# Retention attention and a two-layer product on one core: attention of the later blocks placed at a fixed pace in the plan, smaller groups, another cost for late loads

## The chip, the core and the metric

The kernel runs on one core of a Trainium2 chip. A core has five engines with a queue each: TensorE (PE, matrix products; its weight loads are listed apart as PEld), VectorE (DVE), ScalarE (ACT), GpSimd (POOL) and SyncE (SP), which here issues nearly all transfers between HBM and the on-chip memory SBUF. Products land in PSUM, which this kernel handles as eight banks. Each engine works through its own list in order and waits on semaphores for the others.

The metric is the device time of one execution in microseconds. Before the change the median of three runs is 235.52 us (235.09 to 236.05).

## The reference

Inputs are q, k, v of 4 batches, 8 heads, 768 positions and 64 dimensions, a decay `lam` for each head, and two weight matrices of 512x2048 and 2048x512. Attention is causal without a softmax: position i weighs position j by lam^(i-j). It is written in blocks with a running state:

```python
intra = (qb @ kb.T * Dmask) @ vb                 # Dmask[i,j] = lam**(i-j), i >= j
inter = (qb * lam_pow) @ kv_state
out[block] = intra + inter
kv_state = lam_block * kv_state + (kb * rev_pow).T @ vb
```

The result, as 3072 rows of 512, goes through two products: `h = x @ w_in`, `g = h * sigmoid(h)`, `out = g @ w_out`.

## The kernel before

The 3072 rows are 24 blocks `u` of 128 positions, six to a batch. Per block, attention does this:

- DVE scales q (`qs`, L315) and k (`ks`, L369) by powers of lam; PE transposes both (`tr_ps`, L327 and L389); ACT or DVE copies the transposes to SBUF (`qT`, `kTz`). Except for blocks 0, 1, 22 and 23 (`plain`), q is loaded and scaled for two blocks together, in two halves.
- PE makes the scores (`st_ps`, L415, two halves of four heads), and DVE masks them (`st_sb`, L424).
- v is copied into a padded tile (`vz`). PE makes the block's output (`x_ps`, L453, and L457 for the part from the state), ACT or DVE copies it to `xt`.
- Unless the block ends a batch, PE makes the state's increment (`d_ps`), DVE adds the state (`y`, L500), POOL decays it (`Xz`, `Xf`, L229).

Blocks below `WIDE` = 8 use a padded form of k (`kp`, L361): eight transposes into 128x1024 (L377) with one copy of 1024 columns, eight d_ps products of 64 columns (L480) and one y. The others use four transposes, two copies of 512 columns on 64 partitions, four d_ps products of 128 columns (L484) and two y.

The products work on groups of blocks: `xts[g]` holds one, two or four blocks. The first product (L545) of a group streams 128 columns per block, so 128, 256 or 512; each bank of four 128x128 tiles takes one SiLU on ACT (`g`, L554). A group of any size takes 64 first products. The second product (L573) takes 16 products of 512 columns for each block and needs the whole group's `g` and all of w_out. DVE or ACT copies the result (`o_sb`, L226 and L224) and SP stores it. The last block's second product is split in two halves of 256 columns (L612).

The weights arrive in eight pieces each (`wst`, L269 and L272) and are cast to bf16 on DVE or ACT (`w_in_bf`, `w_out_bf`). SP issues all loads in one written order: k, q, v of the first blocks, w_in between blocks 1 and 6, then w_out, then blocks 8 to 23.

What order each engine's list has is decided at build time by a planner (`Plan`). Every step is an `op` with the engines that may do it and a cost for each, the steps it depends on, a priority, and rings of buffers that it takes and frees. `run` repeatedly takes the step that can start first by its own clock, with fixed latencies between engines, and the instructions are then written out by those start times. The planner's times do not exist at run time: an engine starts an instruction when its semaphores allow it. `after` adds a delay to the time at which a step's dependencies count as done. The step `late`, a step on no engine, makes a load count as landed 4.0 us later for blocks from 8 on. Where the planner sees PE idle in the first 90 us for long enough, `idle` puts in products of zeros (`warm_ps`, L650).

Of the kernel before, what the change touches and what calls it, by code (L numbers as in the profile page):

```python
# [13 lines left out]
class Plan:  # L14
# [9 lines left out]
        self.ops = []  # L24
        self.rings = {}

    def op(self, engines, deps, fn, prio, alloc=(), frees=(), after=0.0):


        o = dict(engines=engines, deps=[d for d in deps if d is not None], fn=fn, prio=prio,  # L30
                 alloc=list(alloc), frees=list(frees), id=len(self.ops), end=None, slots={}, after=after)
        self.ops.append(o)
        return o

# [12 lines left out]
    def run(self, start, idle=None):  # L47
        INF = float("inf")
        free = dict(start)
        users = {}  # L50
        for o in self.ops:
            o["wait"] = len(o["deps"])
            for d in o["deps"]:
                users.setdefault(d["id"], []).append(o)
        ready = [o for o in self.ops if o["wait"] == 0]
        out = []
        while ready:
            pick = {}
            for o in ready:
                slots = max([self.slot(a)[1] for a in o["alloc"]] or [0.0])  # L60
                if slots == INF:
                    continue
                if "SP" in o["engines"]:
                    slots += self.AHEAD
                at = {e: max([free[e] if e != "NONE" else 0.0, slots] + [o["after"] + d["end"] + (self.LAT[d["eng"]] if d["eng"] != e else 0.0)
                                                 for d in o["deps"]]) for e in o["engines"]}
                home = next(iter(at))
                e = min(at, key=lambda e: at[e] + o["engines"][e] + (self.AWAY if e != home else 0.0))
                pick.setdefault(e, []).append((at[e], o))
            if not pick:  # L70
                raise RuntimeError("no operation can start")

            e, l = min(pick.items(), key=lambda kv: min(x[0] for x in kv[1]))
            t0 = min(x[0] for x in l)
            t, o = min((x for x in l if x[0] <= t0 + 0.02), key=lambda x: (x[1]["prio"], x[0], x[1]["id"]))
            if idle is not None and e == "PE":
                idle(free[e], t, out)
            o["eng"], o["start"], o["end"] = e, t, t + o["engines"][e]
            free[e] = o["end"]
            for a in o["alloc"]:  # L80
                i, _ = self.slot(a)
                o["slots"][a] = i
                self.rings[a]["next"] += 1
                self.rings[a]["free"][i] = INF
            for owner, a in o["frees"]:
                self.rings[a]["free"][owner["slots"][a]] = o["end"] + self.LAT[e]
            ready.remove(o)
            out.append((t - (self.AHEAD if e == "SP" else 0.0), len(out), o))
            for u in users.get(o["id"], ()):
                u["wait"] -= 1  # L90
                if u["wait"] == 0:
                    ready.append(u)
        left = [o for o in self.ops if o["end"] is None]
        if left:
            raise RuntimeError(f"{len(left)} operations never start")
        return sorted(out, key=lambda x: x[:2])
# [3 lines left out]
def kernel(  # L100
# [15 lines left out]
    NU = B * NB  # L116
# [4 lines left out]
    KI = DM // 128  # L121
    KO = DFF // 128
    HB = BLK // 2
    WIDE = 8

    ctx.enter_context(tc.manual_schedule())
    const = ctx.enter_context(tc.tile_pool(name="const", bufs=1))
# [3 lines left out]
    plan = Plan()  # L131
# [9 lines left out]
    def sb(o, name, shape, dtype, tag=None):  # L141
        return work.tile(shape, dtype, tag=tag or name, bufs=BUFS[tag or name], name=name)

    def bank(o, name, shape, dtype):
        return ps.tile(shape, dtype, tag=f"b{o['slots']['bank']}", name=name + "_ps")
# [65 lines left out]
    w_in_r = moe_w_in.rearrange("(ko p) f -> p ko f", p=128)  # L211
    w_out_r = moe_w_out.rearrange("(ko p) f -> p ko f", p=128)

    groups = [[0, 1], [2, 3], [4], [5], [6, 7]] + [list(range(u, u + 4)) for u in range(8, NU, 4)]
    group_of = {u: (g, i) for g, us in enumerate(groups) for i, u in enumerate(us)}
    xts = [const.tile([128, KI, len(us) * BLK], BF16, name=f"xt{g}") for g, us in enumerate(groups)]

    plain = {0, 1, NU - 2, NU - 1}

    val = {}  # L220

    def copy(o, dst, src):
        if o["eng"] == "ACT":
            nc.scalar.activation(dst, src, AF.Copy)  # L224
        else:
            (nc.vector if o["eng"] == "DVE" else nc.gpsimd).tensor_copy(dst, src)  # L226
# [20 lines left out]
    for n, (kind, j) in enumerate(order):  # L247
# [28 lines left out]
        o = plan.op({"SP": us}, [prev], fn, n, alloc=[tag])  # L276
        o["tag"] = tag
        load[kind, j] = prev = o
    at = {key: n for n, key in enumerate(order)}
# [17 lines left out]
    def attention(u):  # L297
# [4 lines left out]
        if u in plain or u % 2 == 0:  # L302
            two = u not in plain
            lq = load["q", u]
            late = []
            if u >= 8:
                late = [plan.op({"NONE": 0.0}, [lq], lambda o: None, 0, after=4.0)]
            halves = []
            for t in range(2 if two else 1):
                def fn(o, t=t, first=(t == 0)):  # L310
                    qf = val["qf", u]
                    if first:
                        val["qs", u] = sb(o, "qs", [128, 2, H, 64], BF16)
                    src = qf.rearrange("p h (t d) -> p h t d", t=2)[:, :, t, :] if two else qf
                    nc.vector.tensor_tensor(  # L315
                        val["qs", u][:, t], src,
                        lam_fwd[:, 1 + t if two else 0, :, None].to_broadcast([128, H, 64]), op=AL.mult)
                halves.append(plan.op(
                    {"DVE": 0.7}, [lq] + late + halves[:1], fn, pr + 0.1, alloc=["qs"] if t == 0 else [],
                    frees=[(lq, lq["tag"])] if t == two else []))  # L320
            trs = []
            for t in range(len(halves)):
                def fn(o, t=t):
                    if t == 0:
                        val["trq", u] = bank(o, "tr", [128, len(halves), NP, BLK], BF16)
                    for i in range(NP):
                        nc.tensor.transpose(val["trq", u][:, t, i, :], val["qs", u][:, t, 2 * i:2 * i + 2, :], ident)  # L327
                trs.append(plan.op({"PE": 0.225}, [halves[t]] + trs[:1], fn, pr + 0.1,
                                   alloc=["bank", "n_tr"] if t == 0 else [],
                                   frees=[(halves[0], "qs")] if t == len(halves) - 1 else []))  # L330
            evs = []
            for t in range(len(halves)):
                def fn(o, t=t):
                    if t == 0:
                        val["qT", u] = sb(o, "qT", [128, 2, NP, BLK], BF16)
                    copy(o, val["qT", u][:, t], val["trq", u][:, t])
                evs.append(plan.op({"ACT": 0.6, "DVE": 0.69}, [trs[t]] + evs[:1], fn, pr + 0.1,
                                   alloc=["qT"] if t == 0 else [],
                                   frees=[(trs[0], "bank"), (trs[0], "n_tr")] if t == len(halves) - 1 else []))
            O["qT", u] = evs  # L340
            if two:
                O["qT", u + 1] = evs
# [8 lines left out]

        lk, lv = load["k", u], load["v", u]
        late = []
        if u >= 8:
            late = [plan.op({"NONE": 0.0}, [lv], lambda o: None, 0, after=4.0)]

        wide = u < WIDE
        if wide:
# [14 lines left out]
        if wide:  # L373
# [6 lines left out]
            def fn(o):  # L380
# [3 lines left out]
                          frees=[(tk, "bank"), (tk, "n_tr")])]  # L384
        else:
# [6 lines left out]
            for hh in range(2):  # L392
                def fn(o, hh=hh):
                    if hh == 0:
# [4 lines left out]
                                  alloc=["kTz"] if hh == 0 else [],  # L399
                                  frees=[(tk, "bank"), (tk, "n_tr")] if hh else []))  # L400
# [9 lines left out]
        for half in range(2):  # L410
            def fn(o, half=half):
                val["st", u, half] = bank(o, "st", [128, 4, BLK], F32)
                for i in range(4):
# [5 lines left out]
                         alloc=["bank", "n_st"])  # L419

            def fn(o, half=half):
# [6 lines left out]
                                 frees=[(st, "bank"), (st, "n_st")]))  # L428
# [16 lines left out]
        def fn(o):  # L445
# [4 lines left out]
            for p in range(NP):  # L450
# [5 lines left out]
                if blk > 0:  # L456
                    nc.tensor.matmul(x[:, p, :], lhsT=val["Xz", u][:, p, :], rhs=qT(p), start=False, stop=True)  # L457
        oo = plan.op({"PE": 0.0556 * (8 if blk == 0 else 12)}, masks + [vc] + prev_x + ([O["out", u - 1]] if u else []), fn, pr + 0.4,
                     alloc=["bank", "n_x"], frees=gives)
# [14 lines left out]
        def fn(o):  # L474
            d = bank(o, "d", [128, NP, 64 if wide else 128], F32)
            val["d", u] = d
            for p in range(NP):
# [5 lines left out]
                else:  # L483
# [4 lines left out]
                     alloc=["bank", "n_d"], frees=[(ks, ring_k)])  # L488
        ys = []
        for hh in range(1 if wide else 2):  # L490
            r = slice(0, 128) if wide else slice(64 * hh, 64 * hh + 64)

            def fn(o, hh=hh, r=r):
# [11 lines left out]
                alloc=["y"] if hh == 0 else [],  # L505
                frees=([(dd, "bank"), (dd, "n_d")] + ([(O["Xf", u][0], "Xf")] if blk > 0 else [])) if last else []))
        xs = []
        for hh in range(2):
            def fn(o, hh=hh):
                r = slice(64 * hh, 64 * hh + 64)  # L510
                if hh == 0:
# [3 lines left out]
                              frees=[(ys[0], "y")] if hh == 1 and blk == NB - 2 else []))  # L515
# [7 lines left out]
        O["vz", u] = (vc, oo, dd)  # L523

    for u in range(NU):
        attention(u)
    for vc, oo, dd in (O["vz", u] for u in range(NU) if ("vz", u) in O):
        done = plan.op({"NONE": 0.0}, [oo, dd], lambda o: None, 0, frees=[(vc, "vz")])

# [156 lines left out]
```

## Time and profile before

| what | value |
|---|---|
| median of three runs | 235.52 us |
| the profiled execution, its own time | 237.28 us |
| its span in the trace | 235.6 us |
| PE busy | 221.8 us, 94% |
| DVE, ACT, POOL busy | 114.7, 121.9, 53.1 us |
| first products (L545), second products (L573) | 88.9, 83.3 us busy |
| last PE instruction ends | 232.26 us |
| HBM read, written | 27.27, 6.29 MB |

The span runs from the first to the last instruction of the profiled execution; all times "at" some microsecond are counted from its start. Busy time of PE counts a product from its start to its modelled end, and products overlap, so the busy mean of one (379 ns at 512 columns) is longer than the distance between two starts. Idle time in brackets is what an engine spent empty just before an instruction, with the one that ended it.

### The profile page before, as it was taken

The numbers are of one execution on the slowest core, as the hardware profiler recorded it, in microseconds if no ns is written. First come the engines' busy times: TensorE is split into PE (matmuls) and PEld (weight loads), VectorE is DVE, ScalarE is ACT, GpSimd is POOL, SyncE is SP. The second block draws the span as 40 slices with busy tenths as digits, with TensorE's granted clock in tenths as the row PEclk, the third lists the DMA queues.
The fourth block names the chain that finished last, engine by engine and source line by source line (L and its number), as shares of the span: only waits on it lengthen the run. The fifth ranks groups of instructions, "written<-read, shape, count | busy, mean of one in ns | idle before, by whom it ended". The sixth has DMA issues, their size and how long they took to land.

```text
span 235.6 us, 4440 instructions
## 1 busy us (share of the span) xinstructions
PE 221.8 (94%) x1799; PEld 136.3 (58%) x1799; DVE 114.7 (49%) x184; ACT 121.9 (52%) x213; POOL 53.1 (23%) x71
## 2 busy tenths in 40 slices
PE   4889898999999999979999999999999999999994
PEld 1656687899756676746667544444444444444453
DVE  5677755694359999998997211012100111021221
ACT  5585477867777699869976422401275023710000
POOL 7354420340045244642476100000000000000000
PEclk9999999999999999999999999999999999999999
DMA  6999989999999999999200122204400232023232
GB/s 124 237 288 298 294 227 226 296 363 318 221 228 245 255 262 222 233 238 219 46 1 12 35 47 45 45 2 87 92 0 0 45 75 61 0 45 83 56 86 89
DMA packets 73060, 33.85 MB, mean 144 GB/s; under 512 B 55376, under 2 KB 66000, under 8 KB 73040
## 3 DMA queue, kind: packets, MB, share of 16 engines
q1 hardware_dynamic: 72896, 33.50, 60.4%
q8 instruction: 14, 0.23, 0.4%
q10 hardware_dynamic: 144, 0.07, 0.1%
q14 instruction: 6, 0.05, 0.1%
HBM read 27.27 MB, written 6.29 MB: 142 GB/s over the span
## 4 chain that ended last, share of the span: by engine, by line
PE 52%; DVE 2%; DMA 1%; ACT 1%; issue 0%; DVEq 0%
PE o_ps L573 28%; PE h_ps L545 19%; PE x_ps L453 1%; PE st_ps L415 1%; DVE st_sb L424 1%; PE o_ps L612 1%; DMA out_dram<-o_sb 1%; PE x_ps L457 1%; PE d_ps L484 1%; PE tr_ps L327 0%; PE tr_ps L389 0%; DVE ks L369 0%; DVE y L500 0%; ACT kTz L224 0%; DVE o_sb L226 0%
## 5 line engine op out<-in xcount | busy, mean ns | idle before, releaser
L545 PE MATMUL h_ps<-xt,w_in_bf 128*128 128x512 bf16 (+2 forms) x576 | 88.9, 308 | 0.0
L554 ACT ACTIVATE g<-h_ps 128x512 bf16<-128x512 f32 x96 | 56.3, 597 | 59.2 <-PE h_ps L545 33.0
L573 PE MATMUL o_ps<-w_out_bf,g 128*128 128x512 bf16 x368 | 83.3, 379 | 0.5 <-DVE st_sb L424 0.5
L545 PEld LDWEIGHTS <-w_in_bf 128*128 128x128 bf16 x576 | 49.7, 98 | 29.1 <-DVE w_in_bf L226 0.3
L226 DVE COPY o_sb<-o_ps 128x512 f32<-128x512 f32 (+2 forms) x24 | 15.9, 663 | 87.1 <-PE o_ps L573 84.5
L573 PEld LDWEIGHTS <-g 128*128 128x128 bf16 x368 | 35.2, 98 | 39.6 <-issue 0.7
L229 POOL TENSOR_TENSOR Xz<-y,lam_blk 64x256 bf16<-64x256 f32 x40 | 34.3, 858 | 75.0 <-DVE y L500 46.0
L424 DVE TENSOR_TENSOR st_sb<-st_ps,mask 128x512 bf16<-128x512 f32 x48 | 30.9, 683 | 6.0 <-PE st_ps L415 5.7
L224 ACT ACTIVATE kTz<-tr_ps 64x512 bf16<-64x512 bf16 (+1 forms) x38 | 25.8, 680 | 6.6 <-PE tr_ps L377 2.2
L315 DVE TENSOR_TENSOR qs<-qf,lam_fwd 128x512 bf16<-128x512 f32 x24 | 20.2, 861 | 5.0 <-DMA qf<-in_q_dram 5.0
L224 ACT ACTIVATE xt<-x_ps 128x512 bf16<-128x512 f32 x24 | 14.2, 594 | 9.2 <-PE x_ps L457 8.8
L453 PE MATMUL x_ps<-st_sb,vz 128*128 128x128 bf16 x192 | 18.0, 219 | 0.2
L453 PEld LDWEIGHTS <-vz 128*128 128x128 bf16 x192 | 15.1, 98 | 5.4 <-issue 1.2
L500 DVE TENSOR_TENSOR y<-d_ps,Xf 64x256 f32<-64x256 f32 (+1 forms) x27 | 11.3, 419 | 9.9 <-issue 7.6
L415 PE MATMUL st_ps<-qT,kTz 128*128 128x128 bf16 x192 | 15.1, 222 | 0.5 <-ACT qT L224 0.3
L224 ACT ACTIVATE qT<-tr_ps 128x512 bf16<-128x512 bf16 x22 | 12.8, 594 | 4.4 <-PE tr_ps L327 4.3
L229 POOL TENSOR_TENSOR Xf<-y,lam_blk 128x256 f32<-128x256 f32 x16 | 14.5, 909 | 1.3
L457 PE MATMUL x_ps<-qT,Xz 128*128 128x128 bf16 x80 | 14.5, 219 | 0.0
L415 PEld LDWEIGHTS <-kTz 128*128 128x128 bf16 x192 | 12.5, 99 | 3.1 <-ACT kTz L224 1.0
L224 ACT ACTIVATE o_sb<-o_ps 128x512 f32<-128x512 f32 (+1 forms) x2 | 0.9, 438 | 25.6 <-DMA out_dram<-o_sb 25.6
L369 DVE TENSOR_TENSOR ks<-kf,lam_bwd 128x512 bf16<-128x512 f32 x16 | 14.0, 879 | 0.3
L327 PE MATMUL tr_ps<-ident,qs 128*128 128x128 bf16 x96 | 9.1, 223 | 4.0 <-DVE qs L315 3.8
(54 smaller groups left out, 115.8 us busy)
## 6 DMA issues: line engine op xcount, KB each, us to landing
kf<-in_k_dram SPq DMA_DIRECT2D x24, 256.0 KB, 5.5
vf<-in_v_dram SPq DMA_DIRECT2D x24, 256.0 KB, 5.3
out_dram<-o_sb SPq DMA_DIRECT2D x41, 128.0 KB, 2.4
qf<-in_q_dram SPq DMA_DIRECT2D x10, 512.0 KB, 5.9
wst<-in_moe_w_in_dram SPq DMA_DIRECT2D x8, 512.0 KB, 6.9
wst<-in_moe_w_out_dram SPq DMA_DIRECT2D x8, 512.0 KB, 7.3
qf<-in_q_dram SPq DMA_DIRECT2D x4, 256.0 KB, 5.1
out_dram<-o_sb SPq DMA_DIRECT2D x3, 256.0 KB, 3.6
```

The lines of the kernel that those rows point to most:

```text
L224: nc.scalar.activation(dst, src, AF.Copy)
L226: (nc.vector if o["eng"] == "DVE" else nc.gpsimd).tensor_copy(dst, src)
L229: (nc.vector if o["eng"] == "DVE" else nc.gpsimd).tensor_tensor(dst, a, b, op=op)
L315: nc.vector.tensor_tensor(val["qs", u][:, t], src, lam_fwd[:, 1 + t if two else 0, :, None].to_broadcast([128, H, 64]), op=AL.mult)
L369: nc.vector.tensor_tensor(val["ks", u], val["kf", u], lam_bwd[:, :, None].to_broadcast([128, H, 64]), op=AL.mult)
L415: nc.tensor.matmul(val["st", u, half][:, i, :], lhsT=val["kTz", u][:, h // 2, h % 2, :], rhs=qT(h // 2), start=True, stop=True)
L424: nc.vector.tensor_tensor(val["st_sb", u, half], val["st", u, half], m[:, None, :].to_broadcast([128, 4, BLK]), op=AL.mult)
L453: nc.tensor.matmul(x[:, p, :], lhsT=vp[:, p, hh, :], rhs=val["st_sb", u, h // 4][:, h % 4, :], start=(hh == 0), stop=(hh == 1 and blk == 0))
L457: nc.tensor.matmul(x[:, p, :], lhsT=val["Xz", u][:, p, :], rhs=qT(p), start=False, stop=True)
L545: nc.tensor.matmul(t[:, j, :], lhsT=w_in_bf[:, ko, (m * per + j) * 128:(m * per + j + 1) * 128], rhs=xts[g][:, ko, :], start=(ko == 0), st ...
L554: nc.scalar.activation(t, val["h", g, m], AF.Silu)
L573: nc.tensor.matmul(val["o", u], lhsT=val["g", g, ko][:, i * BLK:(i + 1) * BLK], rhs=w_out_bf[:, ko, :], start=(ko == 0), stop=(ko == KO - 1))
```

## The change

Five edits; no arithmetic changes.

- `Plan.op` takes a time `at` before which the planner doesn't start the step.
- `WIDE` is 4: blocks 4 to 7 use the form of k that blocks from 8 on use.
- Blocks 8 to 11 are two groups of two in place of one of four.
- `late` now also holds for blocks 4 to 7, with 1.2 us; for blocks from 8 on it is 2.0 us in place of 4.0, and no earlier than `pace(u)` = 57 + 5.5 (u - 8) us by the planner's clock.
- PE's steps of attention from block 8 on count their dependencies as done 0.8 us later.

```diff
-    def op(self, engines, deps, fn, prio, alloc=(), frees=(), after=0.0):
+    def op(self, engines, deps, fn, prio, alloc=(), frees=(), after=0.0, at=0.0):
...
-                at = {e: max([free[e] if e != "NONE" else 0.0, slots] + [o["after"] + d["end"] + (self.LAT[d["eng"]] if d["eng"] != e else 0.0)
+                at = {e: max([free[e] if e != "NONE" else 0.0, slots, o["at"]] + [o["after"] + d["end"] + (self.LAT[d["eng"]] if d["eng"] != e else 0.0)
...
-    WIDE = 8
+    WIDE = 4
...
-    groups = [[0, 1], [2, 3], [4], [5], [6, 7]] + [list(range(u, u + 4)) for u in range(8, NU, 4)]
+    groups = [[0, 1], [2, 3], [4], [5], [6, 7], [8, 9], [10, 11]] + [list(range(u, u + 4)) for u in range(12, NU, 4)]
...
+    def pace(u):
+
+        return 0.0 if u < 8 else 57.0 + 5.5 * (u - 8)
...
-            if u >= 8:
-                late = [plan.op({"NONE": 0.0}, [lq], lambda o: None, 0, after=4.0)]
+            if u >= 4:
+                late = [plan.op({"NONE": 0.0}, [lq], lambda o: None, 0, after=2.0 if u >= 8 else 1.2, at=pace(u))]
...
-        if u >= 8:
-            late = [plan.op({"NONE": 0.0}, [lv], lambda o: None, 0, after=4.0)]
+        if u >= 4:
+            late = [plan.op({"NONE": 0.0}, [lv], lambda o: None, 0, after=2.0 if u >= 8 else 1.2, at=pace(u))]
...
     for u in range(NU):
+        n = len(plan.ops)
         attention(u)
+        if u >= 8:
+
+            for o in plan.ops[n:]:
+                if "PE" in o["engines"]:
+                    o["after"] = 0.8
```

The padded k tiles (`kp`) keep their three buffers, and the order of the loads on SP is the same in both kernels; where the stores stand between them differs.

More of the change, by code (lines that the diff above doesn't have):

```diff
@@ L25, in __init__ @@
         self.rings = {}
-    def op(self, engines, deps, fn, prio, alloc=(), frees=(), after=0.0):
+    def op(self, engines, deps, fn, prio, alloc=(), frees=(), after=0.0, at=0.0):
         o = dict(engines=engines, deps=[d for d in deps if d is not None], fn=fn, prio=prio,
-                 alloc=list(alloc), frees=list(frees), id=len(self.ops), end=None, slots={}, after=after)
+                 alloc=list(alloc), frees=list(frees), id=len(self.ops), end=None, slots={}, after=after, at=at)
         self.ops.append(o)
```

## The prediction

> **What bounds the kernel now.** I read the engine shares first, then windows by stage, then the waits of TensorE (PE), then the timeline around each hole.
>
> ```profile
> PE 221.8 (94%) x1799; PEld 136.3 (58%) x1799; DVE 114.7 (49%) x184; ACT 121.9 (52%) x213; POOL 53.1 (23%) x71
> PE   4889898999999999979999999999999999999994
> DVE  5677755694359999998997211012100111021221
> PEclk9999999999999999999999999999999999999999
> ```
> PE is the bound, at full clock. DVE is full only in the middle third, where attention is packed; afterwards it is almost idle.
>
> ```profile
> 20.70:29.83 9.13, 7.70 (x83) 5.77 (x80) 6.43 (x11) 5.37 (x9) 3.10 (x3) 1.00 1.06 306
> 29.83:63.33 33.50, 31.74 (x428) 29.58 (x429) 20.88 (x33) 24.65 (x40) 6.51 (x8) 1.00 1.03 275
> 63.33:89.00 25.67, 25.29 (x254) 16.85 (x252) 21.19 (x33) 20.07 (x37) 9.88 (x11) 1.00 1.07 247
> 89.00:134.00 45.00, 43.15 (x428) 28.79 (x426) 38.70 (x63) 34.41 (x64) 21.78 (x25) 1.00 0.64 130
> 134.00:232.30 98.30, 98.25 (x472) 45.88 (x469) 12.88 (x20) 24.66 (x43) 0.00 (x0) 1.00 0.22 50
> ```
> Columns: window and length, then busy of PE, weight loads, DVE, ACT, POOL, clock, DMA share, GB/s. After 134 us PE never stops, so a microsecond of hole or work removed earlier moves the end by a microsecond. Until 63 us DMA is full, and its landings make the holes:
>
> ```profile
> 29.83 0.40 PE L327 MATMUL tr_ps<-ident,qs 128*128 128x128 bf16 x4 [1.30 <-DVE qs L315]
> 40.71 0.40 PE L327 MATMUL tr_ps<-ident,qs 128*128 128x128 bf16 x4 [1.00 <-DVE qs L315]
> 47.39 0.41 PE L480 MATMUL d_ps<-vz,kp 128*128 128x64 bf16 x8 [0.75 <-DVE vz L226]
> 78.74 0.40 PE L327 MATMUL tr_ps<-ident,qs 128*128 128x128 bf16 x4 [0.30 <-DVE qs L315]
> 103.45 0.40 PE L484 MATMUL d_ps<-vz,ks 128*128 128x128 bf16 x4 [1.39 <-DVE vz L226]
> 120.73 1.02 PE L573 MATMUL o_ps<-w_out_bf,g 128*128 128x512 bf16 x4 [0.46 <-DVE st_sb L424]
> ```
> Start, length, operation, and in brackets PE's idle time just before and who ended it. The first three wait for loads (q of block 4, q of block 6, v of block 7), the last three for a DVE that is behind.
>
> Busy spans overlap in the pipe, so I price PE work by issue distance, from the timeline and the chain: 512 columns 0.216 us (64 in 13.81), 256 columns 0.109 (16 in 1.75), 128 columns 0.056 (8 in 0.45), eight 64-column d_ps products 0.24. Work between two starts, subtracted from their distance, is the true idle: 29.83 to 63.33 holds 31.36 us of work, so 2.14 idle (1.75 of it shown); 63.33 to 133.63 holds 67.18, so 3.12 idle (2.15 shown). With the 1.30 at 28.5 that is 6.56 us after the start-up; the start-up itself (both orders are alike up to the third group of first products, 28.4 us) keeps its idle.
>
> **The change part by part.** Only `WIDE`, `groups`, `late` and `after` differ; the rest is what the planner's order makes of them. I compared both orders engine by engine.
>
> *PE work.* Blocks 4 to 7 take four K transposes instead of eight: 16 x 0.056 = -0.90. Their state products d (three blocks; block 5 ends a batch) go from eight at 64 columns (0.24) to four at 128 (0.22): -0.05. Blocks 8 to 11 as two groups of two: 128 first products at 0.109 instead of 64 at 0.216, +0.13. Two more warm-up products, 2 x 0.216 = +0.43. Sum -0.39. The narrower K also costs ACT two copies of 0.588 for one of 1.024, and DVE two y of 0.418 for one of 0.421; ACT was busy 24.65 of 33.50 us there and DVE 20.88, so +0.15 and +0.42 per block are covered; if that cover went, 4 x 0.57 = 2.3 us would be the ceiling.
>
> *Loads of blocks 4 to 7 counted later.* This moves first products ahead of what waits for loads; the load order on SP stays as it is, so I take the landings of before: q4 29.06, w_in part 7 36.27, q6 39.94, v7 46.24. (1) Two first products (1.74 us) now precede q4's transposes: PE comes at 30.11, the second qs half is done at 30.37 plus 0.07. Hole 1.30 becomes 0.07: -1.23. (2) q6's transposes come after two more products, at about 41.4; qs ends 41.25. -1.00. (3) Block 7's d moves behind the first products of blocks 4 and 5, to about 52.3. -0.75.
> New waits: (4) DVE now has the cast of w_in part 7 before both masks of block 4, and PE has a first product that needs it before block 4's output product. PE gets there at about 35.9 (30.11 plus eight transposes, six products at 0.87, eight narrow ones and eight scores), the cast ends at 36.27 + 0.69 = 36.97: a hole of 1.1. Queued behind the cast are the masks and block 5's ks; the masks then end 38.3, the output product comes at 38.8. Bounds 0 (PE later by my error) to 1.1; I take 1.13, since the landing is a row. (5) Casts of w_out now stand before the masks of blocks 6 and 7 on DVE. The first lands 47.58, cast to 48.3, masks to 49.6; PE needs them at 49.5: +0.15 (0 to 1.4, were the landing one 1.35 us step later). (6) Block 7's output product is now the last work before the group of 6 and 7, so its eviction (0.60) is bare, less 0.43 of warm-up already counted, plus latency: +0.35. Of the 0.39 of small idle I drop 0.20. Together -1.55 (ends: -3.4, if items 4 to 6 and all small idle vanish, and +0.7, if holes 1 and 2 return).
>
> *Attention of 8 to 23 at 5.5 us a block.* Between block 8's and block 23's output products PE's work rises from 58.4 to 80.7 us (second products move in from the tail, at no cost), while DVE's stays at 58 to 59 us (the masks at 0.683, ks and qs at 0.88 and 0.86, y at 0.418 and evictions at 0.69 that stand between these points in either order). So DVE goes from 99% to 73% of PE's work and ACT, about 60, to 74%. The planner's 0.7 for ks and qs is 0.2 too low; packed, that adds up over blocks, at 5.5 us a block the spare 1.4 absorbs it. The 2.15 of shown holes go; of the 0.97 small ones I keep 0.70. -2.42. No row shows the spread order, so the ends are 0 idle left (-3.1) and more idle than before (+2.4, by the worst row, 1.39, four times); I take near the first, because after 134 us, where DVE has slack, idle is nil.
> Queues: SP's loads from block 14 on wait for ks six blocks earlier, and output stores stand behind them. The first stores held so are due about 107, 122 us; three o_sb buffers and at most one eviction waiting cover it. POOL's 2.6 us per block fits 5.5. ACT is tightest between the output products of blocks 9 and 10, about 9.6 us beside 9.6 of PE; three h banks cover the 0.6 to 1.2 it may trail.
>
> The row that could speak against spreading is DVE beside POOL: qs takes 0.69 alone and up to 1.218 beside a POOL product. At 1.22 for both qs and ks a block costs DVE 1.22 x 2 + 1.37 + 0.84 + 0.55 (evictions, casts) = 5.2 us, still under 5.5.
> The Trainium skill (SBUF — State Buffer, "SBUF: two separate sides") says that a DVE operation with two SBUF inputs and a GpSimd operation hold their shared ports in turn for a whole instruction, the other fully blocked. If both then waited out a full POOL product, by its 0.86 row 0.69 + 0.86 = 1.55 each, a block would take 5.9, DVE would be the bound at 5.5, and 16 x 0.4 = 6 us would be lost, ending near 237.5. The means of 0.89 and 0.93 in the packed stretch, where POOL was as busy, show such full waits as rare.
>
> Sum: -0.39 - 1.55 - 2.42 = -4.36. The profiled execution took 237.28 us, its span 235.6; PE ends at 232.26, and the last eviction and store (3.3) are untouched. So 232.9 on its scale. The median of the runs, 235.52, is 1.76 lower; carried over, 231.2 us.
>
> **The rivals.**
> A. The loads still decide until 63 us: the holes of 2.98 are only moved. For: DMA share is 1.03 there, and item 4 is such a case. Against: PE has first products for all of them. Time: 235.52 - 0.39 - 2.42 + 0.07 = about 232.8.
> B. Spreading gives nothing, 3.12 idle stays: masks and vz come late for reasons other than a full DVE. 235.52 - 0.39 - 1.55 = 233.6. Against: 103.45 follows a DVE that had no pause.
> C. No change that can be measured (both A and B): 235.52 - 0.39 = 235.1. A difference under 0.5%, 1.2 us, is what this kernel's runs cannot tell from none.
> D. Slower: each attention step now stands between products, and PE meets it in order; DVE's in-order queue has an eviction of a second product, or a 1.22 qs, before the mask PE wants. A wait of 0.69 + 1.22 = 1.9 against a cover of 0.8 plus one chunk of 0.87 leaves 0.24 twice a block, 7.7 us over 16 blocks against 3.12 now: 235.52 - 1.94 + 4.6 = 238.2. It decides from 0.39 us a block (3.12 + 1.94 + 1.2 over 16). Against: 0.2 a block now, with DVE full.
>
> **How the numbers follow.** Forecast 0.62 (229.8 to 232.4), A 0.14, B 0.10, C 0.06, D 0.08. Faster by over 0.5% (under 234.3) 0.86, same 0.06, slower 0.08. The range 229.8 to 233.8 takes in the forecast with all stretch idle gone at its low end, and A and B; C and D (0.14) are out.
>
> **What would show it.** Right: holes at 30, 40 and 47 us gone; one near 36 of about 1 us ended by a DVE cast of w_in; a short one near 53; DVE's row of tenths at 6 to 8 until about 145 in place of 9; PE idle between 61 and 150 under 1 us; attention's last product about 150. Wrong, if PE waits many times for st_sb or ks after 60 us, if ACT holds the h banks near 75, or if DMA waits outlast 63 us.

## The result and the profile after

The changed kernel takes 231.43 us (median of four runs, 231.25 to 231.73) against 235.38 us beside it (235.09 to 236.05): a ratio of 0.983, 95% interval 0.9806 to 0.9853. Forecast were 231.2 us and a range of 229.8 to 233.8. A second set of runs of the same two kernels gave 231.6 and 235.5, ratio 0.9833. The profiled execution took 231.73 us, with a span of 230.0. Ratios leave out executions in a slower state, of which there was one in all: 235.69 us, with the late loads alone.

The page of the changed kernel, engine shares and the span in 40 slices:

```profile
PE 221.5 (96%) x1837; PEld 142.6 (62%) x1837; DVE 114.0 (50%) x186; ACT 122.0 (53%) x218; POOL 51.7 (22%) x71
...
PE   4989999999999999999999999999999999999994
...
DVE  5676767786479567777828397410110210021221
```

The stretch of 9s on DVE is gone; it now works mostly at 5 to 8 tenths, up to slice 26, 150 us. PE's row has no 7 or 8 left after the start. By stages (window, length, busy of PE, weight loads, DVE, ACT, POOL, clock, DMA share, GB/s), again the changed kernel:

```profile
27.00:63.00 36.00, 35.75 (x444) 32.23 (x442) 24.07 (x39) 28.91 (x52) 6.78 (x8) 1.00 1.06 281
63.00:152.00 89.00, 88.76 (x830) 60.92 (x829) 60.48 (x97) 59.54 (x109) 30.24 (x36) 1.00 0.65 143
152.00:226.70 74.70, 74.70 (x362) 35.24 (x360) 10.11 (x15) 17.34 (x31) 0.00 (x0) 1.00 0.24 55
```

DVE does 60.48 us of work in 89, 68%. What PE still waits for after the start-up, from the timeline of the changed kernel:

```profile
53.17 1.03 PE L555 MATMUL h_ps<-xt,w_in_bf 128*128 128x256 bf16 x8 [0.25 <-ACT xt L228]
...
74.86 0.38 PE L331 MATMUL tr_ps<-ident,qs 128*128 128x128 bf16 x4 [0.15 <-DVE qT L230]
```

Those two are all that the timeline lists between 27 and 152 us, where the kernel before had six.

Busy spans overlap, so I counted true idle as in the prediction: the distance from PE's first start to its last, less the issue distances of all its instructions (0.216, 0.109, 0.056 and 0.03 us for 512, 256, 128 and padded 64 columns).

| profiled execution | its time | PE work | PE idle | to 27 us | 27 to 63 us | after 63 us |
|---|---|---|---|---|---|---|
| before, first trace | 237.28 | 214.97 | 15.75 | 9.04 | 3.61 | 3.11 |
| before, second trace | 235.92 | 214.97 | 14.40 | about 8.8 | about 2.7 | about 2.9 |
| changed, first trace | 231.73 | 214.60 | 10.58 | 9.54 | 0.45 | 0.61 |
| changed, second trace | 231.48 | 214.60 | 10.32 | 9.12 | 0.62 | 0.60 |

Work fell by 0.37 us, idle by 5.2 between the first traces and 4.1 between the second ones. Idle is the remainder of PE's stretch after work, so the two add up to that stretch by construction; what the table shows is that the time outside it is the same in all four (6.56, 6.55, 6.55, 6.56), and where the idle lies. The second trace of before lacks 23 PE records of 512 columns. Each shows as 0.22 us too much between its neighbours, 3, 1 and 19 of them by stage; with these counted as work its stage values are estimates.

### The profile page after: what moved, and what is told of

Read it like the earlier page. It is cut to its first block, busy times and chain, and to the rows that moved or that the text cites. A ratio compares the mean times of both kernels' runs of the same rounds, so it can differ in the third digit from the quotient of the medians.

```text
span 230.0 us, 4541 instructions
## 1 busy us (share of the span) xinstructions
PE 221.5 (96%) x1837; PEld 142.6 (62%) x1837; DVE 114.0 (50%) x186; ACT 122.0 (53%) x218; POOL 51.7 (22%) x71
## 4 chain that ended last, share of the span: by engine, by line
PE 65%; DMA 1%; ACT 0%; DVE 0%; issue 0%
PE o_ps L583 30%; PE h_ps L555 24%; PE x_ps L457 3%; PE st_ps L419 3%; PE tr_ps L331 1%; PE tr_ps L393 1%; PE x_ps L461 1%; PE d_ps L488 1%; PE o_ps L622 1%; DMA out_dram<-o_sb 1%; ACT qT L228 0%; DVE o_sb L230 0%; ACT o_sb L228 0%; ACT xt L228 0%
## 5 line engine op out<-in xcount | busy, mean ns | idle before, releaser
L555 PE MATMUL h_ps<-xt,w_in_bf 128*128 128x256 bf16 (+2 forms) x640 | 91.2, 294 | 0.3 <-ACT xt L228 0.3
L583 PE MATMUL o_ps<-w_out_bf,g 128*128 128x512 bf16 x368 | 84.8, 379 | 0.0
L555 PEld LDWEIGHTS <-w_in_bf 128*128 128x128 bf16 x640 | 55.8, 98 | 22.8 <-PE warm_ps L660 0.6
L233 POOL TENSOR_TENSOR Xz<-y,lam_blk 64x256 bf16<-64x256 f32 x40 | 33.0, 825 | 88.6 <-DVE y L504 42.1
L428 DVE TENSOR_TENSOR st_sb<-st_ps,mask 128x512 bf16<-128x512 f32 x48 | 32.2, 687 | 20.2 <-PE st_ps L419 19.8
L419 PE MATMUL st_ps<-qT,kTz 128*128 128x128 bf16 x192 | 17.4, 223 | 0.4
L419 PEld LDWEIGHTS <-kTz 128*128 128x128 bf16 x192 | 13.7, 100 | 5.9 <-ACT qT L228 0.6
L504 DVE TENSOR_TENSOR y<-d_ps,Xf 64x256 f32<-64x256 f32 (+1 forms) x29 | 12.2, 419 | 7.8 <-PE d_ps L488 4.2
L373 DVE TENSOR_TENSOR ks<-kf,lam_bwd 128x512 bf16<-128x512 f32 x20 | 14.9, 744 | 1.4 <-DMA kf<-in_k_dram 1.2
L228 ACT ACTIVATE vz<-vf 128x512 bf16<-128x512 f32 x20 | 12.5, 627 | 2.9 <-DMA vf<-in_v_dram 2.8
```

Source lines behind the costliest of these rows:

```text
L233: (nc.vector if o["eng"] == "DVE" else nc.gpsimd).tensor_tensor(dst, a, b, op=op)
L373: nc.vector.tensor_tensor(val["ks", u], val["kf", u], lam_bwd[:, :, None].to_broadcast([128, H, 64]), op=AL.mult)
L419: nc.tensor.matmul(val["st", u, half][:, i, :], lhsT=val["kTz", u][:, h // 2, h % 2, :], rhs=qT(h // 2), start=True, stop=True)
L428: nc.vector.tensor_tensor(val["st_sb", u, half], val["st", u, half], m[:, None, :].to_broadcast([128, 4, BLK]), op=AL.mult)
L555: nc.tensor.matmul(t[:, j, :], lhsT=w_in_bf[:, ko, (m * per + j) * 128:(m * per + j + 1) * 128], rhs=xts[g][:, ko, :], start=(ko == 0), st ...
L583: nc.tensor.matmul(val["o", u], lhsT=val["g", g, ko][:, i * BLK:(i + 1) * BLK], rhs=w_out_bf[:, ko, :], start=(ko == 0), stop=(ko == KO - 1))
```

## The experiments

The parts were first run alone, then taken out of the whole, then the pace was varied. Ratios are against runs of the kernel before on the same chip. Its median was 235.2 us beside the three parts alone, 235.5 beside the changed kernel's second runs, those without cover or small groups and the pace of 3.6, 235.4 beside the two parts and the pace of 4.5, and 236.2 beside the last pair, where ratios are therefore the better guide.

**The spread alone.**

```diff
 (against the changed kernel)
-    WIDE = 4
+    WIDE = 8
-    groups = [[0, 1], [2, 3], [4], [5], [6, 7], [8, 9], [10, 11]] + [list(range(u, u + 4)) for u in range(12, NU, 4)]
+    groups = [[0, 1], [2, 3], [4], [5], [6, 7]] + [list(range(u, u + 4)) for u in range(8, NU, 4)]
-            if u >= 4:      # both places of `late`
+            if u >= 8:
```

> The kernel before with the pace, the 2.0 us and the 0.8 us for blocks from 8 on alone; blocks 4 to 7, WIDE and the groups as before. Theory (the packed attention of blocks 8 to 23 leaves PE 3.1 us idle after 63 us, spreading it leaves 0.6; the holes at 28, 40 and 47 us stay): 235.4 - 2.5 = 232.9, and an idle time of PE of 0.6 us after 63 us. Rival (the gain came from the loads of blocks 4 to 7 and the groups; spreading only moves waits): within 0.5 us of 235.4.

233.25 us, ratio 0.9914 (0.9898 to 0.9931), 1.95 us faster. Its timeline lists these waits between 25 and 152 us:

```profile
29.26 0.40 PE L331 MATMUL tr_ps<-ident,qs 128*128 128x128 bf16 x4 [1.21 <-DVE qs L319]
39.88 0.40 PE L331 MATMUL tr_ps<-ident,qs 128*128 128x128 bf16 x4 [0.76 <-DVE qs L319]
45.96 0.41 PE L484 MATMUL d_ps<-vz,kp 128*128 128x64 bf16 x8 [0.15 <-DVE vz L230]
108.09 0.38 PE L331 MATMUL tr_ps<-ident,qs 128*128 128x128 bf16 x4 [0.20 <-ACT qT L228]
```

The holes of the loads stand, those of the packed stretch have gone but for 0.20. Idle after 63 us, with the records that this trace lacks counted as above, is about 0.6, as expected. The theory holds; the gain was 0.5 less than expected (interval 1.6 to 2.4).

**The late loads alone.**

```diff
 (against the kernel before, both places of `late`)
-            if u >= 8:
-                late = [plan.op(..., after=4.0)]
+            if u >= 4:
+                late = [plan.op(..., after=4.0 if u >= 8 else 1.2)]
```

> The kernel before with the loads of blocks 4 to 7 counted 1.2 us late, and nothing else. Theory (first products moved ahead of q4, q6 and v7 fill holes that held 3.5 us of true idle; after 63 us nothing changes): 235.4 - 2.5 = 232.9, holes at 28, 40 and 47 us gone. Rival (transfers bound this stretch, holes only move): above 234.9.

233.78 us, ratio 0.9922 (0.989 to 0.9954). The three holes went, but its timeline has a new one, the wait that the prediction priced at 1.1 us as item 4:

```profile
36.27 1.48 PE L545 MATMUL h_ps<-xt,w_in_bf 128*128 128x256 bf16 x12 [0.74 <-DVE w_in_bf L226]
...
35.52 0.69 DVE L226 CAST w_in_bf<-wst 128x1024 bf16<-128x1024 f32 x1 [1.68 <-DMA wst<-in_moe_w_in_dram]
36.12 1.28 DVE L424 TENSOR_TENSOR st_sb<-st_ps,mask 128x512 bf16<-128x512 f32 x2
```

The first line is PE's, the others DVE's: the cast waits for its piece of w_in to land, with the masks of block 4 behind it, and PE's first product waits for the cast. So the loads do decide part of this stretch, between theory and rival: 1.4 us by the medians and 1.8 by the ratio of the expected 2.5. And not all of it is the holes of the loads: by the same count idle from 27 to 63 us is about 1.6, and after 63 us, where nothing was to change, about 1.8 in place of 2.9 to 3.1.

**Unpadded k for blocks 4 to 7 alone.**

```diff
 (against the kernel before)
-    WIDE = 8
+    WIDE = 4
```

> The kernel before with WIDE = 4 and nothing else: 28 PE instructions fewer, 0.94 us of PE work by issue distance. Theory (PE bound after 134 us, holes stay as they wait for loads): 235.4 - 0.9 = 234.5. Rival (the padded form's longer copies cause the holes): 232 or less. Second rival (the freed work only widens the holes, since the next load ends them): 235.4.

233.88 us, ratio 0.9943 (0.9912 to 0.9975): 1.3 us, the theory's 0.9 lies inside the interval. The first hole stays (1.02 listed at 29.5 us), the second is 0.27, the third is absent; some waits of 0.26 are new. Here too the packed stretch changed with the order: idle after 63 us is about 1.5, and the hole of 1.39 at 103 us is gone, though only blocks 4 to 7 were touched.

**The kernel before, a second trace.**

> The kernel before, unchanged, for a second trace of it. The first trace had w_in part 7 land at 36.27 us and 6.7 us of true PE idle after 28 us; its span fell by 5.6 us with the change, but the median by only 3.95. If the first trace was a slow draw, its second shows that landing at about 34.5 us, as in the changed kernel's trace, and 1 to 1.6 us less idle or a span of about 234. If not, the same holes and 235.6.

235.92 us, span 234.2. The piece of w_in landed at 35.41 us, not 36.27, and the holes were smaller:

```profile
29.55 0.40 PE L327 MATMUL tr_ps<-ident,qs 128*128 128x128 bf16 x4 [1.24 <-DVE qs L315]
40.01 0.40 PE L327 MATMUL tr_ps<-ident,qs 128*128 128x128 bf16 x4 [0.61 <-DVE qs L315]
77.38 0.40 PE L327 MATMUL tr_ps<-ident,qs 128*128 128x128 bf16 x4 [0.30 <-DVE qs L315]
102.10 0.40 PE L484 MATMUL d_ps<-vz,ks 128*128 128x128 bf16 x4 [1.39 <-DVE vz L226]
```

The holes for q6 and v7, which wait for transfers, were 1.00 and 0.75 in the first trace and are 0.61 and unlisted here; the holes of the packed stretch came back to the hundredth (0.30, 1.39). Of the 1.35 us of idle between the two traces about 0.9 lies between 27 and 63 us: the first trace was a slower draw of the loads. The landing of 34.5 that the expectation gave for this case did not come, 35.41 is between the two.

**The changed kernel again, and without its parts.**

> The changed kernel, unchanged, as the mark for the other three and for a second trace: 231.4. In the first trace w_in part 7 landed at 34.50 us and the wait that I had priced at 1.1 us was absent; PE needs the cast at 36.3. If landings of 35.4 to 36.3, as in the four traces of the other orders, come back here, the wait is 0 to 0.7 us before the first product near 36 us; if the changed order itself brings the landing forward, it is 34.5 again.

231.6 us. The piece landed at 35.35 us, so the order of the changed kernel does not bring it forward as such; its cast ran from 35.38 to 36.23, and PE, which started this group's products at 35.90 with the other pieces, went on without a listed wait. After 36.27, the latest landing seen, the cast would end near 37.0 and PE would have waited some 0.7, an estimate.

```diff
-                    o["after"] = 0.8
+                    o["after"] = 0.0
```

> The changed kernel without the 0.8 us on PE's steps; the pace stays. Theory (it is the pace that keeps DVE from being full, the 0.8 us only covers the planner's 0.2 us too low costs): 0.3 to 0.9 us slower than the changed kernel, 231.7 to 232.3. Rival (the 0.8 us is what removes PE's waits): 2 us or more slower, 233.4.

231.19 us, ratio 0.9831 (0.98 to 0.9862), as the whole. Both expectations missed: with this pace the 0.8 us are worth nothing that can be measured. The profile, of the slowest of the four (232.41 us), has 0.27 us of idle after 63 us, less than with the cover, but 2.3 between 27 and 63 us, where the changed kernel has 0.45 and 0.62; 0.60 of it is a wait at 59.9 for q of block 8, which is now asked for earlier.

```diff
-    groups = [[0, 1], [2, 3], [4], [5], [6, 7], [8, 9], [10, 11]] + [list(range(u, u + 4)) for u in range(12, NU, 4)]
+    groups = [[0, 1], [2, 3], [4], [5], [6, 7]] + [list(range(u, u + 4)) for u in range(8, NU, 4)]
```

> The changed kernel with blocks 8 to 11 as one group of four. Theory (second products of eight blocks, 27.6 us, are there to stand between attention until that group is whole, so the smaller groups only cost 0.13 us of PE work): 231.3, no difference that can be measured. Rival (PE runs out of products between 61 and 85 us without them): 1 us or more slower, with idle PE there.

231.6 us, ratio 0.9843 (0.9821 to 0.9864). No difference: the smaller groups carry none of the gain.

```diff
 (against the changed kernel; the groups as in the run above)
-    WIDE = 4
+    WIDE = 8
```

> The changed kernel with WIDE = 8 and one group of four for blocks 8 to 11, so the later loads and the pace alone. If the parts simply add (-1.95 and -1.4 alone): 235.4 - 3.35 = 232.0. If padded k gives the whole only its PE work (0.9 us less two warm-up products, 0.5) and the wait for the cast of w_in part 7, 0.9 us in the trace with late loads alone, stands here too: 231.5 + 0.5 + 0.9 = 232.9. If padded k gives nothing in the whole: 231.5.

232.46 us (231.88 to 234.11), ratio 0.9891 (0.9843 to 0.994). It lies between the first two cases and the interval takes in both. Its trace lists no wait between 25 and 152 us: the last piece of w_in landed there at 34.02, earliest of all, so the wait of the second case could not show. What unpadded k adds to the whole, about 1 us with a wide interval, is not split further.

**The pace.**

```diff
-        return 0.0 if u < 8 else 57.0 + 5.5 * (u - 8)
+        return 0.0 if u < 8 else 57.0 + 3.6 * (u - 8)
```

> The changed kernel with the pace at 3.6 us a block in place of 5.5; the 0.8 us stays. DVE then has about 58 us of work in 56 us of PE's between the output products of blocks 8 and 23. Theory (a full DVE makes the holes after 63 us): 1.5 to 2.5 us slower than the changed kernel, 233 to 233.9, and 2 us or more of idle PE after 63 us. Rival (cover, not pace): within 0.5 us of it.

233.99 us, ratio 0.9951 (0.9918 to 0.9984), 2.4 us slower than the whole, with the 0.8 us of cover in place. With the planner's costs as they are, the pace carries the gain, not the cover. By difference PE idled 2.6 us after 63 us. Two of the waits listed there, and one row of DVE:

```profile
91.43 0.40 PE L488 MATMUL d_ps<-vz,ks 128*128 128x128 bf16 x4 [0.40 <-DVE y L504]
92.87 0.38 PE L393 MATMUL tr_ps<-ident,ks 128*128 128x128 bf16 x4 [0.34 <-DVE st_sb L428]
...
112.28 0.69 DVE L373 TENSOR_TENSOR ks<-kf,lam_bwd 128x512 bf16<-128x512 f32 x1 [2.51 <-DMA kf<-in_k_dram]
```

Both are for DVE, and so is a third of 0.49 at 113.74 for a mask, soon after the row of ks. But DVE is not full throughout, as the theory has it: between the output products of blocks 8 and 23 it is busy 48.85 of 59.40 us, 82%, and it waits 0.45, 1.08 and 2.51 us for loads of q and k. At this pace the loads have a part in the loss, which no run separates.

```diff
-        return 0.0 if u < 8 else 57.0 + 3.6 * (u - 8)
+        return 0.0 if u < 8 else 57.0 + 4.5 * (u - 8)
```

> The changed kernel with 4.5 us a block. DVE has about 58 us of work in 66.5 of PE's between the output products of blocks 8 and 23, 88%. If it takes a full DVE to make holes: within 0.5 us of the changed kernel, 231.4 to 232, idle PE after 63 us under 1 us. If the loss grows with DVE's load all along: halfway to the kernel with 3.6 us a block, about 232.7, and 1.5 us idle.

233.8 us, ratio 0.9925 (0.99 to 0.9949). This is as slow as at 3.6, and neither expectation holds: DVE need not be full over the whole stretch. PE idled about 2.9 us after 63 us, with the 23 records that the trace lacks counted as work. Where it happens, PE first and then DVE in the timeline of this kernel:

```profile
96.73 0.38 PE L393 MATMUL tr_ps<-ident,ks 128*128 128x128 bf16 x4 [1.39 <-DVE o_sb L230]
...
89.67 1.22 DVE L373 TENSOR_TENSOR ks<-kf,lam_bwd 128x512 bf16<-128x512 f32 x1
91.52 0.88 DVE L504 TENSOR_TENSOR y<-d_ps,Xf 64x256 f32<-64x256 f32 x2 [0.62 <-POOL Xf L233]
92.42 1.26 DVE L373 TENSOR_TENSOR ks<-kf,lam_bwd 128x512 bf16<-128x512 f32 x1
93.60 2.35 DVE L319 TENSOR_TENSOR qs<-qf,lam_fwd 128x512 bf16<-128x512 f32 x2
95.98 0.69 DVE L230 COPY o_sb<-o_ps 128x512 f32<-128x512 f32 x1
```

Four ks and qs within 7 us take 1.18 to 1.26 us each where the planner has 0.7: 2 us more than planned, on a DVE that has pauses elsewhere. What ends PE's wait is not ks, which is done at 93.68, but the eviction `o_sb` behind the two qs, done at 96.67: in the code it frees a PSUM bank, and a step of transposes takes one. PE waits at the place that the planner gave the transposes. That suggests that not DVE's load but the planner's error is what counts, which the last pair tests; the expectation below puts this wait down to ks itself.

**The planner's cost.**

```diff
-                    {"DVE": 0.7}, [lq] + late + halves[:1], ...
+                    {"DVE": 0.9 if u >= 8 else 0.7}, [lq] + late + halves[:1], ...
...
-        ks = plan.op({"DVE": 0.7}, ...
+        ks = plan.op({"DVE": 0.9 if u >= 8 else 0.7}, ...
```

> The kernel with 4.5 us a block, with the planner's cost of qs and ks at 0.9 in place of 0.7 us from block 8 on. The trace with 4.5 us showed qs and ks at 1.18 to 1.26 beside POOL between 89 and 96 us, an eviction behind them, and PE 1.39 us idle at 96.7 for ks. Theory (the planner places PE's steps too early because it takes these two for 0.7): idle after 63 us falls under 1.5 us, 231.5 to 232.3. Rival (at this pace DVE's backlog is there whatever the planner believes): 233.3 or more.

231.41 us, ratio 0.9816 (0.9771 to 0.9861) in place of 0.9925: all of the loss comes back, at the denser pace. The same window of both, and the row of ks in it, first with the cost of 0.7, then with 0.9 (PE's counts differ because the first trace lacks records, so its busy time is not to be compared):

```profile
63.00:134.00 71.00, 68.36 (x712) 51.24 (x720) 61.58 (x97) 52.10 (x94) 32.27 (x36) 1.00 0.80 172
...
L373 DVE TENSOR_TENSOR ks<-kf,lam_bwd 128x512 bf16<-128x512 f32 x14 | 13.4, 958 | 0.2
```

```profile
63.00:134.00 71.00, 70.80 (x736) 52.36 (x734) 57.58 (x94) 54.35 (x99) 31.66 (x36) 1.00 0.78 173
...
L373 DVE TENSOR_TENSOR ks<-kf,lam_bwd 128x512 bf16<-128x512 f32 x14 | 11.3, 808 | 0.5 <-DMA kf<-in_k_dram 0.3
```

DVE has 94 instructions here in place of 97, and still does 57.58 us of work in 71, 81%; PE's true idle after 63 us is 0.55, as in the changed kernel. The new order also meets POOL less: the mean of ks in this window is 808 ns, against 958 with 0.7. How much of the gain is the later place of PE's steps and how much this, the runs don't separate.

> The kernel before with the planner's cost of qs and ks at 0.9 in place of 0.7 us from block 8 on, no pace. Theory (DVE is full there, an honest cost can only move PE's steps later, which by itself spreads attention a little): 234.2 to 235.2, idle after 63 us 2 to 3 us. Rival (the planner's error alone makes the holes, and the pace only hides it): 233 or less, idle under 1 us.

234.21 us, ratio 0.9908 (0.9876 to 0.9939), which on 235.4 would be 233.2. Idle after 63 us is 1.75, against 3.11 and about 2.9 in the two traces of the kernel before: 1.1 to 1.4 us of the packed stretch's holes go with an honest cost alone, and a wait for a mask remains:

```profile
108.27 1.02 PE L545 MATMUL h_ps<-xt,w_in_bf 128*128 128x512 bf16 x4 [0.71 <-DVE st_sb L424]
```

It lies between the two expectations: the cost is part of it in the packed order. The rest is not separated: DVE waits for loads here too, 0.76, 2.25 and 1.68 us before ks and qs between 89 and 104 us.

Each of these orders is one draw of the planner: a changed cost or pace moves many steps at once. The five orders with 5.5 us a block have 0.2 to 0.9 us of idle after 63 us; those that pack blocks 8 to 23 have 1.5 to 3.1, and the two at 4.5 us have 2.9 and 0.55. Not run were the cost of 0.9 at the paces of 3.6 and 5.5, and the pace with the old 4.0 us of `late`.

## Why the prediction was right

**The bound and the counting.** PE sets the time: what lies outside its stretch is the same to 0.01 us in the four accounts. PE work was forecast at -0.39 and is -0.37. Idle up to 27 us, which the prediction left as it was, rose by 0.50 in the first pair of traces and by about 0.3 in the second.

**Spread, forecast -2.42.** Idle after 63 us went from 3.11 to 0.61, in the second traces from about 2.9 to 0.60, with 0.70 forecast as kept. The part alone gave 1.95 us, and taking the pace down to 3.6 cost 2.4. The size was right; the reason was right only in part. I argued from DVE's load, 99% against 73% of PE's work; by the traces DVE is busy 55.70 of 62.10 us between the output products of blocks 8 and 23 before, 90%, and 55.67 of 82.10 after, 68%. The other half of my argument, the cost of 0.7 for ks and qs, decides at 4.5 us a block, where the loss is whole with it and absent with 0.9 (in an order that also meets POOL less); in the packed order it is 1.1 to 1.4 of some 3 us. Two things I had not weighed: how much a packed order loses depends on the order (about 1.5 and 1.8 us with parts that touch only blocks 4 to 7), so what spreading is worth lies between about 1 and 2.5 us; and at 3.6 us a block DVE waits for loads. Rival B, that spreading gives nothing, and rival D, waits at every attention step, fell with the two short waits left.

**Loads of blocks 4 to 7, forecast -1.55.** Measured, the stretch from 27 to 63 us went from 3.61 to 0.45, in the second traces from about 2.7 to 0.62: more than forecast, by 1.6 and 0.6 us. The holes to be filled held 3.05 listed in the first trace, 1.85 in the second. The new wait of item 4, +1.13, did not come: its landing (36.27) was the latest of the 14 traces, and with the 34.0 to 35.9 of the others the cast is in this order just about in time. PE came to that group at 36.32 and 35.90, near the forecast 35.9, but the terms as written there add up to 36.7; five products stand before it, not six. The wait is real all the same, 0.74 us in the kernel with late loads alone, at a landing of 35.49. Item 6, the bare eviction before the group of 6 and 7, came as forecast: 0.42 us true idle near 53, besides the two warm-up products. Item 5 is not to be seen. Rival A, holes only moved, fell for the whole; in the part alone one hole of 0.74 came in place of three.

**The transfer to the median.** I carried the difference over from a profiled execution that was 1.9 us above its median. Against that trace the sum should have been -5.55 and I had -4.36; between the second traces it was -4.44, between the medians -3.95. The sum came near the median by luck: a pessimistic term for the loads, and a first trace with larger holes than the second, were both in it.

**Queues.** Stores held behind loads, ACT between the output products of blocks 9 and 10, and POOL gave no listed wait, apart from the 0.15 us at 74.86 in ACT's tight stretch, which waited for a DVE copy. Attention's last product came at 151, as forecast.

## What to carry to other kernels

Where a planner fixes each engine's order, an operation that it takes for 0.2 to 0.5 us too short can show as a stall on the engine that waits while the slow one still has pauses: compare its costs with the row of the busy stretch before spreading or padding the plan. Correcting the cost gave here, at a pace of 4.5 us, what the slower pace of 5.5 us gave without it. And a hole that waits for a transfer should be read from two traces, since its size is partly that of one draw. The same goes for the order: a change of a few steps gave the planner another order, and moved holes far from where it was made.

## What the runs showed of the hardware

The same transfer, the last piece of w_in, issued at 28.3 to 29.2 us in all kernels, landed between 34.02 and 36.27 us over the 14 traces, in identical programs at 36.27 and 35.41, and 34.50 and 35.35.

ks and qs on DVE, with two operands in SBUF, take 0.69 us with no POOL product beside them and up to 1.26 with one, while masks, which read one operand from PSUM, stay at means of 0.683 to 0.689 in either order, beside POOL too. This agrees with the Trainium skill (SBUF — State Buffer, "SBUF: two separate sides"), which has a DVE operation with two SBUF inputs and a GpSimd operation that reads SBUF exclude each other. A full wait for a whole POOL product, 0.72 undisturbed, is not what the rows show: the longest ks is 0.57 above the undisturbed one, and the means of ks after 63 us were 0.73 to 0.96.
